# The last block's first products in column halves, and half of a weight stored to DRAM and loaded back

## The chip, the cores and the metric

The kernel runs on one core of a Trainium2 chip. A core has a matrix engine (TensorE, PE in the profile, with its loads of the stationary operand listed as PEld), a vector engine (VectorE, DVE), an activation engine (ScalarE, ACT), a general engine (GpSimd, POOL) and a queue engine (SyncE, SP) that here only issues DMA transfers. SBUF is the on-chip memory, with 128 partitions. PSUM is the memory into which TensorE writes its sums, with banks of 512 fp32 columns. The metric is device time in microseconds.

## The reference

The input x is 2048 rows of 512. Two branches work on it, and a gate mixes them row by row.

```python
g = sigmoid((x * gate_w).sum(-1, keepdims=True))

# branch a: linear attention, 32 heads of 16
q, k, v = heads(x @ wqkv)
phi(t)  = concat(softmax(t @ w_phi), softmax(-(t @ w_phi)))
kv, z   = phi(k)^T v, phi(k)^T 1
a       = (phi(q) kv / (phi(q) z + 1e-6)) @ wo

# branch b: dense, mish, dense; w1 is 512 x 1376, w2 is 1376 x 512
h = x @ w1 + b1
b = (h * tanh(softplus(h))) @ w2

out = g * a + (1 - g) * b
```

The change lies wholly in branch b.

## The kernel before

Products run in a fast one-pass form (fp32r) on operands that are split in two: a high part and a remainder, called `h` and `l`. One exact product becomes three: high by high, high by low, low by high. So w1, w2 and wo lie in SBUF twice each, as a high and a low tile.

The first part of the program, "A", goes over x in eight chunks of 256 rows. It makes the projections, sums keys and values, and writes the raw query projections to DRAM. In between it splits the weights. The weights of branch b come in two parts: `w1a` and `w2a` hold six tiles of 128 hidden units (the sixth also holds the gate's column), `w1b` and `w2b` hold five. `w2b`'s two tiles are `w2bt` (line 301), each 128 partitions by five slices of 512 columns. In part A the same two tiles serve as buffers for other operands, and only then get w2's values.

The second part, "B", goes over the rows in four blocks of 512 (`b_ops`, line 636). In each block, for each of the eleven tiles of hidden units `i`:

- `up{i}` (line 640): 12 products into one PSUM bank of 512 columns, one per 128 of the contraction and per term (high x high, high x low, low x high). The stationary operand is a 128 x 128 tile of w1, the moving operand is x transposed, 512 columns that stand for the block's 512 rows.
- `mi{i}`, `hi{i}` (lines 651, 656): ScalarE applies mish with the bias, then rounds to the high part.
- `lo{i}` (line 660): POOL subtracts, which gives the low part.
- `dn{i}` (line 664; for the last tile `df{t}`): for each of four row tiles, 3 products into that tile's own PSUM bank, which collects over all eleven `i`. The moving operand is a 512-column slice of w2: `w2at` for the first six `i`, `w2bt` for the last five.

Around it run the steps of branch a for the same block. `lq` loads the query projection (`pq`), VectorE makes its features, `mv` moves them over partitions with 16 transfers (`eT<-tt`), `nu` multiplies them with the key-value sums (`num`) and `wo` with the output weights. `LX0` and `LX1` load the next block's x (`xraw`), and `XH`, `XL` split it (`xbh`, `xbl`). `gr`, `ge` and `gg` make the gate. `fi` (line 795) adds both branches and stores the rows.

The order is written out by hand: the texts `BLOCK0`, `BLOCK1` and `BLOCK` (lines 71 to 95) list the steps, `run` (line 209) issues them in that order, and every engine and queue keeps it (`pin`). A `+` marks a step of the next block. The line that says most of the order around the change is this one of `BLOCK`, which block 3 uses:

```python
    up0 mi0 hi0 lo0 gr S2 T2 rS2 D2 m2 de2 rd2 sc2 es2 tr2 up1 mi1 hi1 lo1 up2 mi2 hi2 lo2 dn0 nu0 oh0 ol0
    S3 T3 rS3 D3 m3 de3 rd3 sc3 es3 tr3 lq0+ lq1+ mv1 up3 mi3 hi3 lo3 dn1 up4 mi4 hi4 lo4 dn2
```

`dn` lags two tiles behind `up`, so that TensorE has other products while mish, rounding and subtraction run. DMA transfers are issued by SP, and by POOL where they add to what lies in memory or convert. All matmuls but two kinds are issued through one helper, so that they carry line 111, and activations carry line 131.

Of the kernel before, what the change touches and what calls it, by code (L numbers as in the profile page):

```python
# [9 lines left out]
F32 = mybir.dt.float32  # L10
# [5 lines left out]
P = 128  # L16
# [4 lines left out]
KT = D // P  # L21
NG = 4
SC = 256
NCH = S // SC
RB = 512
NB = S // RB
FA = 736
NFA = 6
FB = 640
NFB = 5  # L30
NF = NFA + NFB
GROW = FA % P
ORDER = [NFA - 1] + list(range(NFA - 1)) + list(range(NFA, NF))
# [37 lines left out]
BLOCK0 = """  # L71
# [8 lines left out]
BLOCK1 = """  # L80
# [7 lines left out]
BLOCK = """  # L88
# [10 lines left out]
def tile_gated_mix(ctx: ExitStack, tc: tile.TileContext, xT, wv, wkT, wqT, bd, w1a, w1b, b1, w2a, w2b, wo, out):  # L99
# [6 lines left out]
    pin = tc.keep_in_program_order  # L106
    SYNC = mybir.DependencyInfo(mybir.DependencyClass.Sync, mybir.DependencyReason.DATA)
    V, G_, A_, Sy = nc.vector, nc.gpsimd, nc.scalar, nc.sync

    def mm(*a, **k):  # L110
        return pin(nc.tensor.matmul(*a, **k))  # L111
# [14 lines left out]
    def psum(name, tag, bufs={"a": 3, "dn": 4, "kv": 1}):  # L126
        nm[0] += 1
        return pp.tile([P, 512], F32, name=f"{name}_{nm[0]}", tag=tag, bufs=bufs[tag])
# [10 lines left out]
    def f32(ap):  # L139
        return ap.bitcast(F32)  # L140
# [39 lines left out]
    ps = psum("warm", "dn")  # L180
# [25 lines left out]
    def at(key, name, fn):  # L206
        steps.setdefault((key, name), []).append(fn)

    def run(text, key, prev=None, nxt=None):
        for w in text.split():  # L210
            k = prev if w.endswith("'") else nxt if w.endswith("+") else "W" if w.endswith("#") else key
            for fn in steps.pop((k, w.rstrip("'+#")), ()):
                fn()
# [318 lines left out]
    def w1_tile(f, x, k):  # L532
        n_, f, n = ("w1a", f, NFA) if f < NFA else ("w1b", f - NFA, NFB)
        return W[n_][0][x][:, (k * n + f) * P : (k * n + f + 1) * P]

    def w2_tile(f, x):
        n_, f = ("w2a", f) if f < NFA else ("w2b", f - NFA)
        return W[n_][0][x][:, f * 512 : (f + 1) * 512]


    xb = {}
    wob = {}

    def x_ops(b, load, split):

        raw = {}
        for h in range(2):
            def ld(h=h):
                raw[h] = k4("xraw", "tx")
                pin(Sy.dma_start(kt(raw[h], SC), xT[2 * b + h]))  # L550

            def xh(h=h):
                if b not in xb:
                    xb[b] = kt(k8("xbh", "xbh"), RB), kt(k8("xbl", "xbl"), RB)
                act(xb[b][0][:, :, h * SC : (h + 1) * SC], kt(raw[h], SC))

            def xl(h=h):
                sl = slice(h * SC, (h + 1) * SC)
                dve[0] = pin(V.tensor_sub(xb[b][1][:, :, sl], kt(raw[h], SC), f32(xb[b][0][:, :, sl])))  # L559

            at(load[0], load[1 + h], ld)
            at(split, f"XH{h}", xh)
            at(split, f"XL{h}", xl)
# [28 lines left out]
    B = {}  # L592
# [43 lines left out]
    def b_ops(b):  # L636
        key = ("B", b)
        U, dn, tts, eTs, num, ohl, io = {}, {}, {}, {}, {}, {}, {}

        def up(i):  # L640
            f = ORDER[i]
            xh, xl = xb[b]
            ps = psum("up", "a")
            n = 0
            for w, a in ((0, xh), (1, xh), (0, xl)):
                for k in range(KT):
                    mm(ps, w1_tile(f, w, k), a[:, k, :], start=(n == 0), stop=(n == 3 * KT - 1))
                    n += 1
            U[i] = {"ps": ps}

        def mi(i):
            f = ORDER[i]
            U[i]["a"] = k2("act", "hl")
            act(U[i]["a"], U[i]["ps"], AF.Mish, bias=b1s[:, f : f + 1])

        def hi(i):
            U[i]["h"] = k2("h", "hl", F32R)
            act(U[i]["h"], U[i]["a"])

        def lo(i):  # L660
            U[i]["l"] = k2("l", "hl", F32R)
            pin(G_.tensor_sub(U[i]["l"], U[i]["a"], f32(U[i]["h"])))  # L662

        def down(i, t):
            if t not in dn:
                dn[t] = psum("down", "dn")
            f = ORDER[i]
            h, l = [U[i][x][:, t * P : (t + 1) * P] for x in "hl"]
            for n, (a, x) in enumerate(((h, 0), (h, 1), (l, 0))):
                mm(dn[t], a, w2_tile(f, x), start=(i == 0 and n == 0), stop=(i == NF - 1 and n == 2))  # L670

        for i in range(NF):
            at(key, f"up{i}", lambda i=i: up(i))
            at(key, f"mi{i}", lambda i=i: mi(i))
            at(key, f"hi{i}", lambda i=i: hi(i))
            at(key, f"lo{i}", lambda i=i: lo(i))
            for t in range(4):
                at(key, f"dn{i}" if i < NF - 1 else f"df{t}", lambda i=i, t=t: down(i, t))
# [134 lines left out]
    for b in range(NB):  # L813
        b_ops(b)
# [71 lines left out]
    for c in FAST[2:]:  # L886
        w = {
            4: ("O3# L5# sl1'", "", "H4# O4# L11# H5#", "O5# L7# z0"),
            5: ("sl1' ldx", "H11# O11# L8# H7# O7# L9#", "", "H8#"),
        }[c]  # L890
        text = SEVEN
        for name, part in zip(("early", "more", "rest", "late"), w):
            text = text.replace(name, part)
# [1 line left out]
    for c, text in ((NCH - 2, NEXT), (NCH - 1, LAST)):  # L895
        run(text, ("A", c), ("A", c - 1), ("B", 0))
    for b in range(NB):
        run((BLOCK0, BLOCK1, BLOCK, BLOCK)[b], ("B", b), ("B", b - 1), ("B", b + 1))
    assert not steps, list(steps)


# [58 lines left out]
```

## Time and profile before

| | |
|---|---|
| median of three runs | 448.83 us (448.78 to 448.94) |
| profiled execution | 448.44 us |
| its span on the core | 446.7 us |
| TensorE busy | 438.3 us, 98% |
| VectorE, ScalarE, POOL busy | 72%, 47%, 36% |
| block 1 starts, block 2, block 3 | about 223, 296, 370 us |

How to read the views. A row of grouped instructions gives the line, the engine, the operation, output and inputs by the program's names, shapes, the count, then the busy time and the mean duration in ns, then the idle time before it. A timeline row gives start and length in us, engine, line, operation, and how many instructions were merged into it. Matmul records overlap, because they are pipelined: what a product costs is the distance from one start to the next. The names of fp32r operands stand as `f32` in TensorE's rows. The plain-f32 products (`fuse`, `kvp`, `num`, `warm`) appear with two records each. Some matmul records are missing from the trace, so a count can be a few per cent low.

### The profile page before, as it was taken

To read this page: it belongs to the slowest core of one execution; us is meant where nothing else is said; L and a number is where in the kernel's file an instruction comes from. 1 tells how busy PE (TensorE), PEld (TensorE's weight loads), DVE (VectorE), ACT (ScalarE), POOL (GpSimd) and SP (SyncE) were. 2 spreads that over 40 slices of the span, in tenths; PEclk is the share of its full clock that TensorE was granted. 3 is DMA by queue.
4 is the path that set the end of the run, shared out by engine and by line. 5 is a ranking of instruction groups with operands and counts; after the bars stand their busy time and mean duration, and the time that the engine had idled before them with its cause. 6 is when DMAs were issued, how large, how long until landed. Compare 5 with 4: busy or idle time off the path is not lost.

```text
span 446.7 us, 7023 instructions
## 1 busy us (share of the span) xinstructions
PE 438.3 (98%) x2748; PEld 357.3 (80%) x2748; DVE 319.6 (72%) x427; ACT 210.9 (47%) x292; POOL 158.6 (36%) x120
## 2 busy tenths in 40 slices
PE   6999999999999999999999999999999999999996
PEld 6888788788888888787878887887887888787885
DVE  3499779888999999799899868386967438701002
ACT  5864644464454837426374443624253544234220
POOL 2297478575667364212022121113212122221211
PEclk9999999999999999999999999999999999999999
DMA  8424739949836101405351241321151302030002
GB/s 279 170 95 160 169 87 217 215 132 292 249 122 176 49 24 31 112 16 140 100 171 49 53 136 48 94 95 47 47 144 48 91 4 95 1 89 6 0 0 94
DMA packets 27320, 46.35 MB, mean 104 GB/s; under 512 B 5908, under 2 KB 14100, under 8 KB 27288
## 3 DMA queue, kind: packets, MB, share of 16 engines
q1 hardware_dynamic: 25528, 39.88, 29.2%
q0 software_dynamic: 1616, 5.77, 6.4%
q8 instruction: 21, 0.34, 0.3%
q10 hardware_dynamic: 144, 0.26, 0.3%
q14 instruction: 11, 0.09, 0.1%
HBM read 23.87 MB, written 13.64 MB: 84 GB/s over the span
## 4 chain that ended last, share of the span: by engine, by line
PE 96%; DMA 1%; DVE 1%; issue 0%; SPq 0%; ACT 0%; ACTq 0%
PE proj L111 28%; PE up L111 27%; PE down L111 27%; PE wo L111 10%; PE num L111 2%; PE kvp L111 1%; DMA wT<-in_wkT_dram 1%; PE fuse L111 1%; DVE io L797 0%; DVE E L297 0%; DVE Sm L281 0%; ACT E L131 0%; PE z L111 0%; SPq L159 0%; DVE Sm L289 0%
## 5 line engine op out<-in xcount | busy, mean ns | idle before, releaser
L662 POOL TENSOR_TENSOR l<-act,h 128x512 fp32r<-128x512 f32 x44 | 60.1, 1367 | 220.7 <-ACT h L131 184.7
L131 ACT ACTIVATE act<-up,b1s 128x512 f32<-128x512 f32 x44 | 30.3, 689 | 87.1 <-PE up L111 86.8
L131 ACT ACTIVATE E<-E 128x1024 f32<-128x1024 f32 x32 | 33.7, 1060 | 48.4 <-DVE E L275 34.3
L297 DVE TENSOR_TENSOR E<-E,Sm 128x1024 f32<-128x1024 f32 x32 | 42.3, 1321 | 1.0
L281 DVE TENSOR_REDUCE Sm<-E 128x64 f32<-128x1024 f32 x32 | 38.7, 1211 | 5.9 <-ACT E L131 5.9
L111 PE MATMUL wo<-woh,ohl 128*128 128x512 f32 x128 | 40.7, 389 | 0.0
L111 PE MATMUL down<-w2ah,h 128*128 128x512 f32 x96 | 37.5, 390 | 0.0
L111 PE MATMUL down<-w2ah,l 128*128 128x512 f32 x96 | 37.4, 389 | 0.0
L111 PE MATMUL down<-w2al,h 128*128 128x512 f32 x96 | 37.3, 389 | 0.0
L797 DVE SCALAR_TENSOR_TENSOR io<-down,og_sb,io 128x512 f32<-128x512 f32 x16 | 11.2, 749 | 31.0 <-PE down L111 31.0
L111 PE MATMUL down<-w2bh,h 128*128 128x512 f32 x80 | 31.2, 390 | 0.0
L111 PE MATMUL down<-w2bl,h 128*128 128x512 f32 x80 | 31.1, 389 | 0.0
L111 PE MATMUL down<-w2bh,l 128*128 128x512 f32 x80 | 31.1, 389 | 0.0
L131 ACT ACT_TABLE_LOAD x20 | 25.7, 1283 | 10.1 <-PE up L111 9.8
L771 DVE TENSOR_TENSOR ohl<-num,ohl 128x512 fp32r<-128x512 f32 x16 | 10.2, 679 | 26.3 <-ACT ohl L131 26.3
L131 ACT ACTIVATE h<-act 128x512 fp32r<-128x512 f32 x44 | 27.8, 632 | 1.4
L111 PEld LDWEIGHTS wo<-woh,ohl 128*128 128x128 f32 x128 | 24.0, 188 | 5.0
L111 PE MATMUL up<-xbh,w1ah 128*128 128x512 f32 x96 | 26.3, 396 | 0.0
L111 PE MATMUL up<-xbh,w1al 128*128 128x512 f32 x96 | 25.7, 389 | 0.0
L111 PE MATMUL up<-xbl,w1ah 128*128 128x512 f32 x96 | 25.7, 389 | 0.0
L559 DVE TENSOR_TENSOR xbl<-xraw,xbh 128x1024 fp32r<-128x1024 f32 x8 | 10.1, 1291 | 21.3 <-ACT xbh L131 21.3
L111 PE MATMUL wo<-wol,ohl 128*128 128x512 f32 x64 | 24.9, 389 | 0.0
(155 smaller groups left out, 1010.9 us busy)
## 6 DMA issues: line engine op xcount, KB each, us to landing
xraw<-in_xT_dram SPq DMA_DIRECT2D x16, 512.0 KB, 5.1
eT<-tt SPq DMA_DIRECT2D x128, 64.0 KB, 2.0
zd<-E POOLq DMA_DIRECT2D x10, 512.0 KB, 7.2
pqd<-qs SPq DMA_DIRECT2D x16, 256.0 KB, 4.3
pq<-pqd SPq DMA_DIRECT2D x16, 256.0 KB, 2.8
out_dram<-io SPq DMA_DIRECT2D x16, 256.0 KB, 2.1
raw<-in_w1a_dram SPq DMA_DIRECT2D x3, 512.0 KB, 4.2
raw<-in_w2a_dram SPq DMA_DIRECT2D x3, 512.0 KB, 4.5
```

Source lines behind the costliest of these rows:

```text
L111: return pin(nc.tensor.matmul(*a, **k))
L131: return pin(A_.activation(out_, in_, fn, **k))
L281: pin(V.tensor_reduce(d["S"], hv(d["E"][:, :]), axis=AX.X, op=ALU.add))
L297: dve[0] = pin(eng.tensor_mul(hv(d["E"][:, :]), hv(d["E"][:, :]), d["S"][:, :, None].to_broadcast([P, 2 * H, DH])))
L559: dve[0] = pin(V.tensor_sub(xb[b][1][:, :, sl], kt(raw[h], SC), f32(xb[b][0][:, :, sl])))
L662: pin(G_.tensor_sub(U[i]["l"], U[i]["a"], f32(U[i]["h"])))
L771: pin(V.tensor_sub(ohl[h, gp][:, 512:], num[h, gp], f32(ohl[h, gp][:, :512])))
L797: pin(V.scalar_tensor_tensor(io[t], dn[t], og_sb[:, i : i + 1], io[t], op0=ALU.mult, op1=ALU.add))
```

## The change

In the last block, each `up{i}` but the first is made in two halves: all 12 products over the first 256 columns, then all 12 over the other 256, into the two halves of the same PSUM bank. Each half loads the same 12 stationary tiles. Mish still reads the whole bank.

Beside that, the last five slices of w2, high and low, are stored to DRAM in block 1 (ten stores of 256 KB on SP's queue, ahead of `up7` in the text) and loaded back in the last block into the tiles where they already are: two loads behind each of `lo1` to `lo5`, issued by POOL, since a load from an f32 tensor into an fp32r tile converts. The values are the same.

```diff
+    w2d = tc.dram_tile([P, 2, NFB * 512], F32, name="w2d")
...
             ps = psum("up", "a")
-            n = 0
-            for w, a in ((0, xh), (1, xh), (0, xl)):
-                for k in range(KT):
-                    mm(ps, w1_tile(f, w, k), a[:, k, :], start=(n == 0), stop=(n == 3 * KT - 1))
-                    n += 1
+            for sl in (slice(0, SC), slice(SC, RB)) if b == NB - 1 and i else (slice(0, RB),):
+                n = 0
+                for w, a in ((0, xh), (1, xh), (0, xl)):
+                    for k in range(KT):
+                        mm(ps[:, sl], w1_tile(f, w, k), a[:, k, sl], start=(n == 0), stop=(n == 3 * KT - 1), skip_group_check=True)
+                        n += 1
...
+        def rl(i):
+            f = ORDER[i] - NFA
+            sl = slice(f * 512, (f + 1) * 512)
+            for x in range(2):
+                if b == 1:
+                    pin(Sy.dma_start(w2d[:, x, sl], f32(w2bt[x][:, sl])))
+                else:
+                    pin(G_.dma_start(w2bt[x][:, sl], w2d[:, x, sl]))
+
         for i in range(NF):
+            if i >= NFA and b in (1, NB - 1):
+                at(key, f"rl{i}", lambda i=i: rl(i))
...
-        run((BLOCK0, BLOCK1, BLOCK, BLOCK)[b], ("B", b), ("B", b - 1), ("B", b + 1))
+        text = (BLOCK0, BLOCK1, BLOCK, BLOCK)[b]
+        if b == 1:
+            text = text.replace("up7", "rl6 rl7 rl8 rl9 rl10 up7")
+        if b == NB - 1:
+            for i in range(6, 11):
+                text = text.replace(f"lo{i - 5} ", f"lo{i - 5} rl{i} ")
+        run(text, ("B", b), ("B", b - 1), ("B", b + 1))
```

## The prediction

> **What bounds the kernel now.** I read the page first (busy shares, granted clock, chain), then the chain of its last 80 us, then the waits of TensorE, then the loads and products of TensorE one by one.
>
> ```profile
> span 446.7 us, 7023 instructions
> PE 438.3 (98%) x2748; PEld 357.3 (80%) x2748; DVE 319.6 (72%) x427; ACT 210.9 (47%) x292; POOL 158.6 (36%) x120
> PEclk9999999999999999999999999999999999999999
> PE 96%; DMA 1%; DVE 1%; issue 0%; SPq 0%; ACT 0%; ACTq 0%
> 392.69 2.72 PE up L111 x12
> 395.42 2.72 PE down L111 x12
> 403.57 2.72 PE up L111 x12
> 410.04 2.94 PE up L111 x12
> 434.74 6.82 PE down L111 x30
> 441.58 0.69 DVE io L797
> PE fuse L111 <- DMA wT<-in_wkT_dram: 2.5, 2, 1.8
> PE warm L111 <- DVE ones L179: 1.1, 1, 1.1
> PE kvp L111 <- DVE E L297: 0.7, 1, 0.7
> PE proj L111 <- issue: 0.2, 1, 0.2
> ```
>
> The chain of work that ended last is TensorE for 96% of the span, at full granted clock throughout. In the last block it goes from one group of products to the next without a gap. The last four rows are all that the list of TensorE's waits holds (us in total, times, longest): 4.5 us, none of it before an `up`, a `down` or a `wo`. So every nanosecond added to the last block's products reaches the end, and whatever happens on another engine counts only if it makes a product wait. Each of the ten `up` groups that the change touches takes 2.72 us for 12 products; the one right after the `num` products shows 2.94, which includes the switch from them.
>
> **The products in halves.** Ten groups (all but the first of the last block) go from 12 products of 512 columns to 24 of 256 columns. The columns multiplied are the same, but loads of the stationary tile and products both double: 120 more of each. What matters is the pitch, the distance from one start to the next, since the records overlap.
>
> ```profile
> L111 PE MATMUL up<-xbl,w1ah 128*128 128x512 f32 x96 | 25.7, 389 | 0.0
> L111 PEld LDWEIGHTS up<-xbl,w1ah 128*128 128x128 f32 x96 | 18.0, 188 | 3.8
> L111 PE MATMUL num<-eT,kvb 64*32 64x256 f32 x256 | 8.8, 382 | 0.0
> L111 PE MATMUL kvp<-E,v 128*32 128x64 f32 x512 | 8.4, 220 | 0.7 <-DVE E L297 0.7
> L111 PEld LDWEIGHTS fuse<-bds,wT 128*128 128x128 f32 x32 | 3.9, 191 | 3.1 <-DMA bds<-in_bd_dram 2.1 <-DMA wT<-in_wkT_dram 0.9
> 10.98 0.27 PE L111 MATMUL fuse<-bds,wT 128*128 128x128 f32 x1
> 11.64 0.39 PE L111 MATMUL fuse<-bds,wT 128*128 128x128 f32 x2
> 10.98 0.19 PEld L111 LDWEIGHTS fuse<-bds,wT 128*128 128x128 f32 x1
> 11.87 0.19 PEld L111 LDWEIGHTS proj<-wkl,xh 128*128 128x128 f32 x1
> 381.52 0.77 PEld L111 LDWEIGHTS up<-xbh,w1ah 128*128 128x128 f32 x4 [0.41 <-issue]
> ```
>
> Now: 2.72 us / 12 = 226.7 ns per product. A load record is 188 ns long, but that is not its pitch. The `fuse` loads of the same 128x128 size, 191 ns long, start at 10.98, and the eighth start after that is at 11.87 us: 0.89 / 8 = 111 ns each, with a product of 128 plain-f32 columns behind each one (10.98 to 11.64, six steps: 110 ns). The `up` loads tell the same: after the switch at 381.52 four loads take 0.77 us; less the last one's 0.188 and two pitches of 0.227, the first step, in which no product runs yet, was 0.77 - 0.188 - 0.453 = 0.129 with the timeline's rounding (other switches give 0.11 to 0.12). So a load needs some 111 to 120 ns, and it runs while the product before it streams. At 512 columns that is hidden with over 100 ns to spare; at 256 columns the cover is nearly as short as the load.
>
> What the 256 columns themselves need is not in this trace: every fp32r product here has 512. It is bounded so. From below: a pair can't come faster than its load, 111 ns, so a group would take 24 x 0.111 = 2.66 us, 0.06 less than now, and ten groups 0.6 us less. From above by the nearest rows: if the whole 188 ns load record stood before each product, 24 x 0.188 = 4.51 us a group and 17.9 us in all; the `fuse` rows, with as long a record and 111 ns of pitch, exclude that nearly.
> Between these: how much of the 226.7 ns belongs to the columns, and how much to each product whatever its size? The plain-f32 rows have several widths: 256 columns 382 ns, 64 columns 220 ns, so (382 - 220) / 192 = 0.844 ns a column. An f32 record of 256 columns is about as long as an fp32r record of 512 (382 to 389), so I take half of that for an fp32r column, 0.422 ns: an estimate from these rows. Then 512 columns are 216.0 ns, and 10.7 ns belong to the product. With 256 columns a product takes 108.0 + 10.7 = 118.7 ns, just above the load's 111. A group: 24 x 118.7 = 2.849 us against 2.72, or 12 x 10.7 = 0.128 us more; ten groups: 1.28 us. I take this value, because 226.7 is measured on the very products that are split, while the 111 ns come from plain-f32 products, whose data stream at half the rate.
>
> On the fixed part the Trainium skill differs: "TensorE: Matmul & The Clock Gate", section "Back-to-back issue gap", gives N / 2.4 + 2.5 ns for a warm product, by which only 2.5 ns are fixed. By that page 512 columns would come every 215.8 ns; this trace has 226.7, so 11 ns are not in its formula, and no run here yet shows whether they go with the product or with the columns. Going by its 2.5 ns the edit would cost 120 x 2.5 ns = 0.3 us.
>
> Who waits for a later `up`: mish, the split and the subtraction follow the whole 512-column tile, as before, so halves give them nothing sooner. They delay nothing either: the `down` products lag two groups behind.
>
> **The stores in block 1.** Ten stores of 256 KB go onto SP's queue, after the two `pq` loads and ahead of the two `xraw` loads and 16 `eT` transfers.
>
> ```profile
> 260.21 1.08 SPq L708 DMA_DIRECT2D pq<-pqd  x2
> 261.40 13.82 SPq L550 DMA_DIRECT2D xraw<-in_xT_dram  x2
> 278.60 10.18 SPq L750 DMA_DIRECT2D eT<-tt  x16
> 295.25 2.37 SPq L798 DMA_DIRECT2D out_dram<-io  x4
> out_dram<-io SPq DMA_DIRECT2D x16, 256.0 KB, 2.1
> xraw<-in_xT_dram SPq DMA_DIRECT2D x16, 512.0 KB, 5.1
> 289.67 1.99 ACT L131 ACTIVATE xbh<-xraw 128x1024 fp32r<-128x1024 f32 x2
> ```
>
> They wait for nothing, as w2 was split long before. An issue takes 2.37 / 4 = 0.59 us by the output's rows, so 5.9 us: the first `xraw` moves from 261.4 to 267.3. Its data are read at 289.67 by ScalarE. If all ten stores went one behind the other at 2.1 us (21 us from 261.4, so to 282.4) and the load's 5.1 us came after them, it would land at 287.5, still in time. The second `xraw` is issued only by 261.40 + 13.82 = 275.2, as now, and `eT` at 278.6 feeds the `num` products of the next block, which stand behind three of its `up` groups. Cost: nothing; covers: the 22 us to 289.67. Without it a late `xraw` would hold the first `up` of block 2 and cost its lateness one for one.
>
> **The loads in block 3.** Two converting loads of 256 KB go onto POOL's queue behind each of the residual subtractions `lo1` to `lo5`.
>
> ```profile
> L454 POOL DMA_DIRECT2D zd<-E x8: 856/872/905, 44.1 to 100.6; - x8
> DMA to landing us min/median/max: 3.0/7.1/9.4
> 377.02 1.63 POOL L662 TENSOR_TENSOR l<-act,h 128x512 fp32r<-128x512 f32 x1 [1.74 <-issue]
> 379.38 1.29 POOL L662 TENSOR_TENSOR l<-act,h 128x512 fp32r<-128x512 f32 x1 [0.73 <-ACT h L131]
> 397.00 1.29 POOL L662 TENSOR_TENSOR l<-act,h 128x512 fp32r<-128x512 f32 x1 [4.15 <-ACT h L131]
> 418.26 0.39 PE L111 MATMUL down<-w2bh,h 128*128 128x512 f32 x1
> 369.69:441.70 72.01, 72.01 (x372) 58.38 (x372) 20.04 (x31) 22.83 (x34) 14.52 (x11) 1.00 0.10 28
> ```
>
> (The last row's columns: stretch, length, busy time and count of PE, PEld, DVE, ACT, POOL, granted clock, DMA share, GB/s.)
>
> The nearest row is the accumulating `zd` transfer: 0.87 us of POOL to issue, 3.0 to 9.4 us to land, for twice the bytes. Ten issues are 8.7 us of POOL, beside 14.5 us of POOL's work in a block of 72 us. The loads have to wait for block 2's last `down` products, which read the same tiles; TensorE ends these before it starts block 3's `up0`, so the wait is over when POOL gets there. Behind the first pair stands `lo2`: it would go from 379.38 to 378.65 + 1.74 = 380.4, and its reader `dn2` stands just ahead of the `up` at 392.69, so at 390.0. The last pair is issued at 398.3 + 1.74 = 400.0 and lands by 409.4; the first reader of any of these tiles is the product at 418.26. Spare: 8.8 us, so I cost it at nothing. From above, should the ten run one behind the other at 9.4 us each, all of 94 us from 378.7, the last would land at 472.7, while its products start two groups after 434.74, at 440.2: 32.5 us.
>
> **Sum.** Profiled execution 448.44 us (446.7 span and 1.7 around it); + 1.28 for the ten groups, + 0 for stores and loads = 449.7. The median of the runs is 448.83, 0.39 above the profiled one; on that scale 450.1 us, 0.29% more.
>
> **The rivals.**
> Not slower: the extra 10.7 ns go with the columns, or the plain-f32 `fuse` pitch holds. For it: `fuse` at 110 to 111 ns streams about as long a product (128 columns x 0.844 = 108 ns) with 3 ns on top. Against it: those columns come at half the rate, so reads have room there. At half of 226.7 the time stays 448.8; at 111 ns it is 448.2; with the skill's 2.5 ns it is 449.1. It decides where the fixed part is under 7.5 ns (0.9 us / 120); under a pitch of 109.6 ns (0.9 us / 240 below 113.3) it would even be faster by 0.2%. Chance 0.28.
> Load and hand-over add up: if the next load starts only when the product's fixed part is over, the pitch is 111 + 10.7 = 121.7 to 120 + 10.7 = 130.7 ns, so 2.92 to 3.14 us a group, 2.0 to 4.2 us in all: 450.8 to 453.0. For it: load and product are of the same length, so neither covers the other's jitter. Against it: after the switches, the load runs beside the product from the start. Chance 0.14.
> The reload is late: a wait at 418.26 takes the place of none. It starts to cost once the last pair needs more than 18 us from its issue to land, and takes up to 32.5 us, as above. Against it: a DMA share of 0.10 in this block and landings of at most 9.4 us for twice the bytes. Chance 0.04.
>
> **How the numbers follow.** The forecast, a fixed part of about 10.7 ns, has 0.54; not slower 0.28; adding up 0.14; late 0.04. About 0.2% (0.9 us) is what a measurement of this kernel can tell from no change. Slower: the forecast and the two above it, less 0.04 for a fixed part that is smaller than taken, 0.68. Faster by over 0.2%: the bottom of the second case, 0.04. The same: 0.28. The range goes from 448.3, near the load's bound, to 452.2, just past the middle of the adding case (450.8 to 453.0); the forecast's own range is 449.6 to 450.6.
>
> **What would show it.** In the changed profile the ten `up` groups of the last block stand with 24 products each of 128x256; 2.85 us a group is the forecast, 2.72 or less the first rival, 2.92 and more the second. TensorE's waits stay empty in the last block; a wait of `down` on `w2bh` or `w2bl` in its row is the third. In block 1 the `xbh` of ScalarE should start at 289.7 as now. I would be wrong if load and product interfere in a way that no row here shows, as at 256 columns the two are equally long for the first time.

## The result

The changed kernel takes 450.97 us (median of seven, 450.52 to 452.28) against 448.8 us (median of seven, 448.12 to 449.51). The ratio is 1.0055, with a 95% interval of 1.0041 to 1.0069: slower by 1.8 to 3.1 us. The forecast was 450.1, and the range 448.3 to 452.2 holds the result, but the cost is nearly twice the 1.28 us forecast. The time lies above the forecast's own range (449.6 to 450.6) and within the one that the prediction gave to its second rival (450.8 to 453.0), so only the parts of the cost can tell which mechanism it was.

The page of the changed kernel, its head and the two chain lines:

```profile
span 450.5 us, 7289 instructions
PE 442.3 (98%) x2868; PEld 366.3 (81%) x2868; DVE 319.0 (71%) x427; ACT 210.9 (47%) x292; POOL 165.4 (37%) x130
PE 96%; DMA 1%; DVE 1%; ACT 0%; issue 0%; ACTq 0%
PE proj L111 28%; PE up L111 27%; PE down L111 26%; PE wo L111 10%; PE fuse L111 2%; PE num L111 2%; PE kvp L111 1%; DMA bds<-in_bd_dram 1%; DVE io L810 0%; DVE E L297 0%; DVE Sm L281 0%; ACT E L131 0%; PE z L111 0%; DVE Sm L289 0%; PE kvT L617 0%
```

TensorE has 120 products and 120 loads more, and it is still 96% of the chain. The chain of the last block in order of time (start, length in us, what) shows where the block became longer:

```profile
371.08 8.47 PE up L111 x60
379.55 2.75 PE down L111 x12
...
389.13 2.87 PE up L111 x24
392.01 2.75 PE down L111 x12
394.75 2.87 PE up L111 x24
397.63 2.75 PE down L111 x12
400.37 5.44 PE wo L111 x24
...
437.82 6.84 PE down L111 x30
444.66 0.02 issue
444.69 0.69 DVE io L810
```

A halved group takes 2.87 us where it took 2.72, and the `down` group behind it 2.75 where it took 2.72. One step of the block, `up` and `down`, is 394.75 - 389.13 = 5.62 us, against 392.69 - 387.25 = 5.44 before (from the chain of the kernel before, whose piece `387.25 2.72 PE up L111 x12` stands one `down` group ahead of the one at 392.69). From the block's first `up` to the first output addition it is 444.69 - 371.08 = 73.61 us, against 441.58 - 369.69 = 71.89: 1.72 us more.

TensorE's waits of the changed kernel, all there are:

```profile
PE fuse L111 <- DMA bds<-in_bd_dram: 1.9, 1, 1.9
PE warm L111 <- DVE ones L179: 1.1, 1, 1.1
PE kvp L111 <- DVE E L297: 0.7, 1, 0.7
```

So no `down` waited for a reloaded slice, and no `up` for a late x. The transfers stand where the prediction put them. GpSimd's loads and SP's transfers, from the timeline:

```profile
400.46 0.56 POOL L681 DMA_DIRECT2D w2bh<-w2d  x1
401.01 0.55 POOL L681 DMA_DIRECT2D w2bl<-w2d  x1
DMA to landing us min/median/max: 3.0/3.7/4.5
420.98 0.40 PE L111 MATMUL down<-w2bh,h 128*128 128x512 f32 x1
268.83 0.60 SPq L679 DMA_DIRECT2D w2d<-w2bl  x1
269.53 7.09 SPq L551 DMA_DIRECT2D xraw<-in_xT_dram  x2
291.07 1.99 ACT L131 ACTIVATE xbh<-xraw 128x1024 fp32r<-128x1024 f32 x2
```

A load costs POOL 0.55 us (0.87 was taken) and lands within 4.5 us; the last is there by 406 us, and the first product that reads one of these slices starts at 420.98. The first `xraw` went from 261.4 to 269.5 (1.4 us of it because this whole execution runs later, as the next paragraph says), and ScalarE still reads x 6.8 us before block 2 starts, as before.

One thing in this profile is not the change's. Its execution took 452.28 us, the longest of the seven, and its block 0 started 1.5 us late (149.76 against 148.25), after slow `fuse` products at the very start, long before the first instruction that the change adds. The kernel with the transfers alone has its block 0 at 147.72.

### The profile page after: what moved, and what is told of

It is laid out like the page before. It is cut to its first block, busy times and chain, and to the rows that moved or that the text cites. A ratio compares the mean times of both kernels' runs of the same rounds, so it can differ in the third digit from the quotient of the medians.

```text
span 450.5 us, 7289 instructions
## 1 busy us (share of the span) xinstructions
PE 442.3 (98%) x2868; PEld 366.3 (81%) x2868; DVE 319.0 (71%) x427; ACT 210.9 (47%) x292; POOL 165.4 (37%) x130
## 4 chain that ended last, share of the span: by engine, by line
PE 96%; DMA 1%; DVE 1%; ACT 0%; issue 0%; ACTq 0%
PE proj L111 28%; PE up L111 27%; PE down L111 26%; PE wo L111 10%; PE fuse L111 2%; PE num L111 2%; PE kvp L111 1%; DMA bds<-in_bd_dram 1%; DVE io L810 0%; DVE E L297 0%; DVE Sm L281 0%; ACT E L131 0%; PE z L111 0%; DVE Sm L289 0%; PE kvT L617 0%
## 5 line engine op out<-in xcount | busy, mean ns | idle before, releaser
L664 POOL TENSOR_TENSOR l<-act,h 128x512 fp32r<-128x512 f32 x44 | 61.9, 1406 | 215.4 <-ACT h L131 163.7
L111 PE MATMUL wo<-woh,ohl 128*128 128x512 f32 x128 | 40.7, 389 | 0.0
L111 PE MATMUL down<-w2ah,h 128*128 128x512 f32 x96 | 37.5, 391 | 0.0
L111 PE MATMUL down<-w2al,h 128*128 128x512 f32 x96 | 37.4, 390 | 0.0
L111 PE MATMUL down<-w2ah,l 128*128 128x512 f32 x96 | 37.4, 389 | 0.0
L111 PE MATMUL down<-w2bh,h 128*128 128x512 f32 x80 | 31.3, 391 | 0.0
L111 PE MATMUL down<-w2bl,h 128*128 128x512 f32 x80 | 31.2, 390 | 0.0
L111 PE MATMUL down<-w2bh,l 128*128 128x512 f32 x80 | 31.1, 389 | 0.0
L111 PEld LDWEIGHTS wo<-woh,ohl 128*128 128x128 f32 x128 | 24.0, 188 | 5.1
L111 PE MATMUL up<-xbh,w1ah 128*128 128x512 f32 (+1 forms) x116 | 27.2, 356 | 0.0
L111 PE MATMUL up<-xbh,w1al 128*128 128x512 f32 (+1 forms) x116 | 26.7, 352 | 0.0
L111 PE MATMUL up<-xbl,w1ah 128*128 128x512 f32 (+1 forms) x116 | 26.7, 352 | 0.0
L111 PE MATMUL wo<-wol,ohl 128*128 128x512 f32 x64 | 24.9, 389 | 0.0
```

## The experiments

**The halves alone.** Without stores and loads.

```diff
-            if i >= NFA and b in (1, NB - 1):
+            if False:
...
-        if b == 1:
-            text = text.replace("up7", "rl6 rl7 rl8 rl9 rl10 up7")
-        if b == NB - 1:
-            for i in range(6, 11):
-                text = text.replace(f"lo{i - 5} ", f"lo{i - 5} rl{i} ")
```

> The halves alone: no stores of w2 in block 1 and no loads in block 3. The changed kernel's profile has 2.87 us for each halved group (2.72 before) and 2.75 for the down group behind it (2.72 before), so 0.18 us for each of ten. Theory H, the halves are the whole cost: 448.8 + 1.8 = 450.6 us, ratio about 1.004, equal to the changed kernel within 0.4 us. Rival T, the transfers cost what the halves do not explain of the measured 2.2 to 2.5 us: this kernel stays at 450.6 and the changed kernel's extra 0.4 to 0.7 us appear in the transfers alone.

Measured: 450.06 us against 448.28 on that chip, ratio 1.0039 (1.0025 to 1.0053). The chain of its last block, first `up` and first output addition:

```profile
369.60 8.47 PE up L111 x60
443.21 0.69 DVE io L809
```

These are 73.61 us apart, exactly the changed kernel's figure. The halves cost 1.72 us, and the rest of the changed kernel's loss isn't theirs.

**The transfers alone.** All `up` groups with 512 columns.

```diff
-            for sl in (slice(0, SC), slice(SC, RB)) if b == NB - 1 and i else (slice(0, RB),):
+            for sl in (slice(0, RB),):
```

> The stores and the converting loads alone, every up group with 512 columns again. Theory H: nothing reaches TensorE, 448.8 us, ratio 1.000 with its interval holding 1. Rival T: 449.2 to 449.5 us, ratio 1.001 to 1.0015, with a gap or longer products of TensorE in block 1 or block 3.

Measured: 449.59 us, ratio 1.0026 (1.0012 to 1.0039), so 0.5 to 1.7 us. Theory H fails: the transfers are not free. But rival T, as I had written it, fails too, since TensorE has no gap and no longer product:

```profile
369.35 8.16 PE up L111 x36
441.24 0.69 DVE io L810
442.65 0.75 DVE io L810
```

From the block's first `up` to the first addition it is 71.89 us, as in the kernel before. The difference comes after the work: the last addition ends at 443.40 and the span at 447.1, so 3.7 us, against 443.75 and 446.7 before, 3.0 us. These 0.7 us lie within the 0.5 to 1.7 of the ratio. This stretch is called the tail below. The rows of the kernel's last line hold what SP does there: a list of nine semaphore checks, then drains and barriers. (A semaphore is a counter that tells of a finished step, here of a transfer that has landed; a check is an instruction that waits for one.) A few of them from the kernel before (durations, first and last start):

```profile
L956 SPq EVENT_SEMAPHORE  x2: 28/28/28, 444.3 to 444.4; - x2
L956 SPq EVENT_SEMAPHORE  x1: 28/28/28, 445.2 to 445.2; - x1
L956 SPq EVENT_SEMAPHORE  x1: 28/28/28, 445.8 to 445.8; - x1
L956 SPq DRAIN  x2: 7/7/7, 445.9 to 446.0; - x2
```

And from the transfers alone:

```profile
L975 SPq EVENT_SEMAPHORE  x1: 28/28/28, 444.8 to 444.8; - x1
L975 SPq EVENT_SEMAPHORE  x1: 28/28/28, 445.5 to 445.5; - x1
L975 SPq EVENT_SEMAPHORE  x1: 28/28/28, 446.0 to 446.0; - x1
L975 SPq EVENT_SEMAPHORE  x1: 28/28/28, 446.2 to 446.2; - x1
L975 SPq DRAIN  x1: 7/7/7, 446.3 to 446.3; - x1
```

Before, SP runs through most checks at 444.2 to 444.5, while the outputs are still on their way. Only the last two have to wait, and the drain follows the last check at once. With the transfers, the checks that wait come first, at 444.8 and 445.5, and six more follow, which take until 446.2. The outputs themselves are no later: the last one lands 2.1 us after the last addition in both (at 445.82 and 445.47), and from there to the end of the span it is 0.9 us before and 1.6 us with the transfers. SP's waits for the outputs in all:

```profile
SPq L956 <- DMA out_dram<-io: 1.2, 2, 0.6
```

```profile
SPq L975 <- DMA out_dram<-io: 1.6, 2, 1.0
```

(the kernel before, then the transfers alone).

The trace records which semaphore each transfer signals and which one each check waits for, and this tells why. SP's transfers use eight semaphores in turn, and the closing list checks the same eight, in the same order in every kernel. The kernel before has 231 transfers on SP, and its last four outputs signal the 5th, 6th, 7th and 8th semaphore of the list. With ten transfers more they signal the 7th, 8th, 1st and 2nd. So the list waits for the last two outputs at its start, and the other six checks still have to be made when the last output has landed. By this account eight transfers more should change nothing, and two should do what ten do. The next runs try that.

**Eight stores in place of ten.** The transfers alone, the same bytes.

```diff
                 if b == 1:
-                    pin(Sy.dma_start(w2d[:, x, sl], f32(w2bt[x][:, sl])))
+                    if f:
+                        so = slice(0, 1024) if f == 1 else sl
+                        pin(Sy.dma_start(w2d[:, x, so], f32(w2bt[x][:, so])))
```

> The transfers alone, with the same bytes stored by eight transfers in place of ten (the first two slices of each half go together); the ten loads stay. In the profiles, the distance from the end of the last output addition of VectorE to the end of the span is 3.7 us in both kernels with transfers and 3.0 us in those without. Theory E, ten more transfers on SP's queue move the outputs to other places in the list of semaphores that SP goes through at the end, which seems to turn round with eight: with eight stores the order is as before, the tail is 3.0 us, the time 448.3 us on the scale of 448.3 and the ratio 1.000. Rival M, more semaphores, packets or the loads on GpSimd make the end longer: 3.7 us again, ratio 1.0016.

Measured: 448.85 us against 448.21, ratio 1.0011 (1.0000 to 1.0022). The rows of its end and of its last addition:

```profile
442.45 0.75 DVE io L812
L977 SPq EVENT_SEMAPHORE  x1: 28/28/28, 444.6 to 444.6; - x1
L977 SPq DRAIN  x1: 7/7/7, 445.3 to 445.3; - x1
```

The span ends at 446.2, 3.0 us after the last addition, and the checks that wait are again the last two; the last four outputs signal the 5th to 8th semaphore. The ratio lies between none and 1 us; a small further cost isn't excluded, but the tail is back as theory E had it, with the ten loads in place.

**Two stores, and ten stores without loads.**

```diff
-            if i >= NFA and b in (1, NB - 1):
+            if i == NFA and b == 1:
...
-            text = text.replace("up7", "rl6 rl7 rl8 rl9 rl10 up7")
+            text = text.replace("up7", "rl6 up7")
```

This is the edit for two stores. The other kernel keeps the line of `up7`. Both leave out the loads, and all `up` groups have 512 columns.

> Only two of the ten stores, and no load: two transfers more on SP's queue than in the kernel before. Theory E: ten and two are the same turn of eight, so the tail from the end of the last output addition to the end of the span is 3.7 us. Rival M (bytes, packets or the loads): 3.0 us, or little above.

> All ten stores, no load. Theory E: the tail is 3.7 us as with the loads. If the loads on GpSimd make the end longer: 3.0 us.

Measured, one execution each: 448.93 and 449.57 us, with tails of 3.5 us (last addition 442.98 + 0.75, span 447.2) and 3.7 us (443.40 + 0.75, span 447.85). Two stores in the middle of the program are enough for most of the longer end, and the loads have no part in it.

| kernel | transfers added on SP | places in the list that the last four outputs signal | from the last addition to the end |
|---|---|---|---|
| before; halves alone; halves in all blocks; the two other cuts | 0 | 5, 6, 7, 8 | 3.0 us each |
| eight stores; the change with eight stores | 8 | 5, 6, 7, 8 | 3.0, 3.0 us |
| two stores | 2 | 7, 8, 1, 2 | 3.5 us |
| ten stores; transfers alone; the changed kernel | 10 | 7, 8, 1, 2 | 3.7 us each |

**The change with eight stores.**

> The changed kernel with eight stores of the same bytes in place of ten. Theory E: the halves' 1.72 us stay and the tail goes back to 3.0 us: 448.3 + 1.75 = 450.05 us, ratio 1.0039, as the halves alone had it. Rival M: 1.0055 as the changed kernel.

Measured: 450.11 us, ratio 1.0045 (1.0027 to 1.0062), tail 3.0 us. The time is what theory E had (450.05), but this interval alone holds both theories' ratios; it is the tail that decides between them.

**Other cuts.** 384 and 128 columns, and four quarters, both without transfers.

```diff
-            for sl in (slice(0, SC), slice(SC, RB)) if b == NB - 1 and i else (slice(0, RB),):
+            for sl in (slice(0, 384), slice(384, RB)) if b == NB - 1 and i else (slice(0, RB),):
# the second kernel:
+            for sl in [slice(o, o + P) for o in range(0, RB, P)] if b == NB - 1 and i else (slice(0, RB),):
```

> Without the transfers; the ten groups are cut into 384 and 128 columns in place of 256 and 256. Theory F, a fixed part of 12.6 ns for each product (a line through 226.7 ns at 512 columns and 119.6 at 256): 384 columns come every 173 ns. Rival L, the pitch goes with the columns (0.443 ns each) and 256 columns came at 119.6 ns because of their load: 384 columns every 170.0 ns. Under both, 128 columns can not go below their load; F has it at the 111 ns that the plain-f32 loads show, L at 119.6 again. A group is then 3.41 us by F and 3.48 by L, against 2.72 before, and the kernel 455.7 or 456.4 us.

> Without the transfers; the ten groups are cut into four quarters of 128 columns, so 48 products and 48 loads each. The load sets the pitch. At 111 ns (F, as the plain-f32 loads had it) a group is 5.33 us and the kernel 448.8 + 26 = 475 us; at 119.6 ns (L) 5.74 us and 479 us. If a quarter's products ran at half rate or each load had to end before its product, the pitch would be 188 ns or more, 9 us a group and over 510 us.

Measured, one execution each: 456.27 and 475.68 us. TensorE's timeline and the chain of the first, then the chain of the second:

```profile
390.38 0.86 PE L111 MATMUL up<-xbh,w1al 128*128 128x384 f32 x4
391.08 0.85 PE L111 MATMUL up<-xbl,w1ah 128*128 128x384 f32 x4
391.78 0.56 PE L111 MATMUL up<-xbh,w1ah 128*128 128x128 f32 x4
396.03 3.40 PE up L111 x24
```

```profile
395.63 5.31 PE up L111 x48
400.94 2.83 PE down L111 x12
```

384 columns: four products from 391.08 to 391.78 are 175 ns each, but these times are rounded to 10 ns. The trace's unrounded starts are 391.083 and 391.776, so 173 ns each, and the median of the run's 110 steps from one such product to the next is 174. F had 173 and L 170. A quarter's product comes every 5.31 / 48 = 110.6 ns. So a load with its product can come every 110.6 ns, and the 119.6 ns at 256 columns are not set by the load. L falls, and a fixed part per product, F, holds. A group of 384 and 128 takes 3.40 us, as F had it (3.41), but the kernel's 456.27 us is nearer to L's 456.4. The difference is behind the halves: the `down` group after short products takes 2.75 us behind 256 columns, 2.80 behind the 128 that end the uneven cut, 2.83 behind quarters. The expectation had left that out.

**The halves in all blocks.**

```diff
-            for sl in (slice(0, SC), slice(SC, RB)) if b == NB - 1 and i else (slice(0, RB),):
+            for sl in (slice(0, SC), slice(SC, RB)):
```

> Without the transfers; all 44 up groups of all four blocks in halves, in place of ten. The cost of a group was 0.15 us for itself and 0.03 for the down group behind it. Theory H: 44 x 0.15 to 0.18 = 6.6 to 7.9 us, so 455.4 to 456.7 us, ratio 1.015 to 1.018. A rival, in blocks 0 to 2 other work stands beside TensorE and hides or adds something: outside of these.

Measured: 455.89 us, ratio 1.0163 (1.0142 to 1.0183), so 7.3 us for 44 groups, 0.166 us a group (0.145 to 0.186 by the interval; 0.172 in the last block). The cost of a group is the same beside the much busier VectorE of the earlier blocks, and TensorE's list of waits has no `up` and no `down`:

```profile
PE fuse L111 <- DMA bds<-in_bd_dram: 1.8, 1, 1.8
PE warm L111 <- DVE ones L179: 1.1, 1, 1.1
PE kvp L111 <- DVE E L297: 0.7, 1, 0.7
```

## Why the prediction was right, and where it was not

The direction was right and mostly for the reason given: each fp32r product carries a part that does not shrink with its columns, and TensorE has no slack in the last block. The size was not: of some 2.4 us, the forecast had 1.28.

*The fixed part.* Forecast 10.7 ns and a group of 2.849 us; the chain has 2.87, so 119.6 ns a product. The line through 512 and 256 columns, (226.7 - 119.6) / 256 = 0.418 ns a column, leaves 12.6 ns. The estimate from the plain-f32 rows (0.422 ns a column) was 1% high in the slope, and a slope's error is taken 512 times. Ten groups: 1.5 us in place of 1.28. That the estimate came so near is partly luck: it is half of a slope between the record lengths, not the pitches, of two other kinds of product.

*The group behind.* The sum had nothing for the `down` groups. They take 0.03 us more behind a halved group, 0.2 to 0.3 us in all. This grows with shorter products in front (0.08 and 0.11 us in the other cuts); in the timeline it is the first products of the group whose steps are longer (0.29 us for the first step behind 128 columns, in place of 0.227). With the 1.5 us it makes the 1.72 us of the block.

*The transfers, "+ 0 for stores and loads".* This is the step that failed. Each cover that I named held: the x loads, the `eT` transfers and the ten loads landed in time and TensorE never waited. I had followed the stores to all that stands behind them on SP's queue but its very end. There the program checks its transfers' eight semaphores one by one in a fixed order. Ten more transfers move the last outputs from the list's last places to its first, so that six checks are left when they have landed, and the end is 0.7 us longer. 1.72 + 0.7 = 2.4 us agrees with the ratio's 1.8 to 3.1. Eight transfers more leave the places and the end as they were, and two change both, so it is the count of the transfers and not their bytes or the loads. That the transfers cost nothing else is not shown to better than some 0.5 us: with eight stores alone the median is 0.6 us above the kernel before, with an interval from 0 to 1.

*The rivals.* "Not slower" is out: each of the 120 products that were added costs 12 to 13 ns. "Load and hand-over add up" was priced at 121.7 to 130.7 ns a product; 119.6 was measured, and quarters at 110.6, less than a load of 111 and a fixed part of 10.7 together, show that load and product do run side by side. That the total came out within this rival's range is a coincidence: the closing checks and the `down` groups brought it there, not the pitch. "The reload is late" had 15 us to spare. The Trainium skill ("TensorE: Matmul & The Clock Gate", section "Back-to-back issue gap") has a fixed 2.5 ns for a warm product, from which the estimate was 120 x 2.5 ns = 0.3 us. It does not hold for these fp32r products: halving them cost 1.5 us in TensorE's own pitch, five times that.

What stays open: in all three ends with ten stores there is a pause of about 0.35 us between two checks (445.6 to 446.0 in the transfers alone) that two stores do not show, and no row says what SP waited for. The transfer that this check asks for had been issued over 45 us earlier. Without the pause the end would be some 0.4 us longer in place of 0.7. Why `down` is slower behind short products isn't shown either.

## What to carry to other kernels

Where TensorE is the bound, as here, splitting a matmul costs its fixed part once per added piece, even if no column is added and the loads fit: get that part from the pitch at two widths, not from record lengths, and test the line at a third. Look for a cost also behind the last useful instruction: the closing checks belong to the time, and a transfer that is added or taken away can move the last outputs to other places among them. Before a difference of under 1 us is put down to the work, compare the distance from the last output to the span's end.

## What was unexpected of the hardware

An fp32r product came every 226.7 ns at 512 columns, 174 at 384, 119.6 at 256 and 110.6 at 128. By the line through 512 and 256 columns, 128 columns would come every 66 ns; 110.6 is the pitch of the `fuse` loads (110 to 111), so the load of the 128 x 128 tile seems to be the limit there. At 256 columns only 9 ns lie between the two limits, so a product with fewer columns can come at most 9 ns sooner. And two stores of 256 KB, 180 us before the end and with nobody waiting for them, made the end of the program 0.5 us longer, in the one execution that was profiled.
